# A fused recurrence and two-layer network: another order of the front, with pad copies first, a copy of x ahead of a copy of v, and a weight request moved up

## The chip, the cores and the metric

The kernel runs on one core of a Trainium2 chip. The metric is the device time of one execution in microseconds. Twelve runs of the kernel before lie between 196.32 and 199.08 us, with a median of 197.39. The engines are named as in the profile: PE is TensorE (PEld its weight loads), DVE is VectorE, ACT is ScalarE, POOL is GpSimd, SP is SyncE, which here only asks for transfers. Times inside an execution are counted from the start of its span.

## The reference

For each of 4 batches and 8 heads a state of 48 x 48 is carried through 768 steps, and its output goes through a network of two layers.

```python
for t in range(S):                                   # B, H, S, D = 4, 8, 768, 48
    kt, vt, rt = k[:, :, t], v[:, :, t], r[:, :, t]
    cur = np.einsum('bhd,bhe->bhde', u[None] * kt, vt)
    y[:, :, t] = np.einsum('bhd,bhde->bhe', rt, state + cur)
    state = w[None, :, :, None] * state + np.einsum('bhd,bhe->bhde', kt, vt)
...
x = y.transpose(0, 2, 1, 3).reshape(B * S, H * D)    # 3072 x 384
h = x @ w_in                                         # 384 x 2048
g = h * (1.0 / (1.0 + np.exp(-h)))
return g @ w_out                                     # 2048 x 384
```

## The kernel before

The sequence is cut into 6 chunks of 128 steps. A unit is one chunk of one batch, so there are 24 units; unit i is batch i mod 4 of chunk i // 4. Units 0 to 3 are chunk 0 and start from an empty state. Units are worked in pairs; the second of a pair is "crossed", which means that its masked products stand with the two halves of the partitions exchanged, and its v has to be copied crossed as well.

For each unit r, k and v are loaded (192 KB each, SP's queue, L73). PE turns r and k by transposes (L255) into a PSUM tile `att`; DVE multiplies them with powers of the decay while it takes them out (rT and kT, L261); PE multiplies them pairwise (L288) and DVE masks the result (am, L295). PE then forms y from am and v, and from the second chunk on from the state too (L305, L310). DVE adds the bonus term vu and writes y in 16 bits (y16, L338). The bonus comes from POOL and DVE: rk = r * k (L215), times u (L220), a sum on DVE (L228), and the product with v on POOL (vu, L233). For the state, POOL multiplies k with the decay to the chunk's end (kc, L223), PE multiplies it with v (sp, L322), and DVE adds the result to the decayed state (sdec on POOL, L333). ScalarE casts v (L242, and two more copies, L245 and L246, for a crossed unit).

The network's first layer needs y turned: PE transposes it (yT, L376) and ScalarE copies it to SBUF (xT, L380). Then come the matmuls with w_in (`hps`, L391), SiLU on ScalarE (L399), the matmuls with w_out (`ops`, L412), and the copy and store of the result. w_in and w_out are loaded as four quarters each by POOL's queue, with a cast to 16 bits (L84, L89); a quarter of w_in covers four of the 16 blocks of 128 hidden units. From chunk 1 on, y is turned by a DMA.

The engines run in the order of the program, each its own instructions one after the other; nothing is rescheduled. For the front (units 0 to 7) the order is written by hand as a string of words, `order` (L489 to L500). Each word issues one step, and all of its instructions go to one engine:

| Word | Step | Engine |
|---|---|---|
| T4 | turn r and k of unit 4 | PE |
| rT4, kT4 | take them out with the decay | DVE |
| A45 | products of units 4 and 5 | PE |
| am4, rd4, y164, st4 | mask, bonus sum, y, state | DVE |
| Y4, S4, yT4 | y, state product, turned y | PE |
| v164, xT4, r164 | casts and copies | ACT |
| rk4, ru4, vu4, kc4, sd4 | bonus products, decayed k, decayed state | POOL |
| L2.6, G2.6 | first layer of chunk 0, a block of batches from 2 on, hidden block 6: matmuls, then SiLU | PE, ACT |
| H0 | first layer of chunk 1, two hidden blocks of batches 0 and 1 | PE, ACT |
| i_q0, i_o0 | request of a quarter of w_in, of w_out | POOL |
| lr4, lk4, lv4 | loads of unit 4 | SP |
| pads | zeros beside the 48 columns of r and k of units 4 to 7: eight copies, L159 | ACT |
| mx, clear, wb | a mask, PSUM cleared, the decay spread | ACT, PE, PE |

A number with a star ahead of a word, as in `3*A23`, first issues so many matmuls on a tile of zeros (`spin`, L165), whose result nobody reads.

The tiles yp, yT, hps, sp, ops and those of `spin` share four PSUM buffers (tag "moe"). A new tile takes the buffer that was released earliest in the program's order: its first matmul waits until the last reader of that buffer is done. In the order before, L0.4 takes the buffer of L0.2 (free after G0.2), L4.8 that of S1 (free after st1), and yT4 that of L4.14.

After the order string a loop (L522 to L574) works the units 6 to 23 in pairs, with pieces of the two layers as fillers between them. The change doesn't touch it.

Of the kernel before, what the change touches and what calls it, by code (L numbers as in the profile page):

```python
# [15 lines left out]
def kernel(  # L16
# [132 lines left out]
    eK = cst.tile([PR, NP, C], FP)  # L149
    lamR = cst.tile([PR, NP, C], FP)  # L150
    lamK = cst.tile([PR, NP, C], FP)
    lnw_bc = cst.tile([128, HD], FP)
    lamC = cst.tile([128, H, D], FP)
# [316 lines left out]
    def piece(word, f):  # L470
# [16 lines left out]
        "lr": lambda i: ld(i, rin, r), "lk": lambda i: ld(i, kin, k), "lv": lambda i: ld(i, vin, v),  # L487
    }
    order = """  # L489
        lnw eK lamK mx clear lr4 lk4 lv4 lr5 lk5 lv5 lr6 lk6 lv6 lr7 lk7 lv7 4*T0 rk0 rT0 kT0  # L490
        1*T1 rT1 kT1 rk1 ru0 rd0 v160 v161 3*A01 wb am0 ru1 vu0 rd1 am1 vu1 lnwb lamC i_q0 1*Y0
        y160 T2 kT2 rT2 2*Y1 rk2 1*yT0 xT0 ru2 3*T3 kT3 rT3 v162 y161 rk3 i_q1 3*A23 v163 pads
        yT1 xT1 ru3 rd2 vu2 rd3 vu3 am2 am3 L0.0 G0.0 L0.2 G0.2 Y2 y162 Y3 y163 kc0 i_q2 yT2 xT2
        L0.4 G0.4 kc1 yT3 xT3 L0.6 G0.6 S0 st0 kc2 T4 kT4 rT4 kc3 L2.0 G2.0 S1 L2.2 G2.2 st1 rk4
        v164 L2.4 G2.4 S2 L2.6 G2.6 st2 ru4 i_q3 r164 L4.8 G4.8 S3 L4.9 G4.9 st3 rd4 rk5 L4.10
        G4.10 T5 kT5 rT5 L4.11 G4.11 vu4 ru5 i_o0 A45 rd5 am4 r165 v165 L4.12 G4.12 vu5 kc4
        L4.13 G4.13 am5 sd4 kc5 Y4 S4 y164 st4 L4.14 G4.14 sd5 i_o1 Y5 S5 y165 st5 L4.15 G4.15
        yT4 xT4 yT5 xT5 T6 kT6 rT6 rk6 ru6 i_o2 H0 H1 v166 r166 H2 H3 T7 kT7 rT7 rk7 i_o3 v167
        r167 H4 ru7 rd6 stb4 stb5
    """  # L500
    for word in order.split():
# [104 lines left out]
```

## Time and profile before

| What | Value |
|---|---|
| Median of 12 runs | 197.39 us (196.32 to 199.08) |
| Profiled execution | 197.65 us |
| Its span, first to last instruction | 195.9 us |
| PE matmuls busy | 184.0 us, 94% of the span |
| ACT busy | 108.6 us, 55% |
| POOL busy | 120.2 us, 61% |
| DVE busy | 102.7 us, 52% |
| Mean granted clock of PE | 0.991 |

The share of PE is a mean over stages that differ. The page gives the span in 40 slices of 4.9 us, each digit a busy share in tenths (9 is 90% or more):

```profile
PE   7897399889999999999999999999999999999994
PEld 2645277557866886665556665556655556644563
DVE  6696339784664563663772782782673464200120
ACT  5391667767744276067685066793186791179300
POOL 8779962799999966937928919919827630000000
PEclk9999889999999999999999999999999999999999
DMA  5999989899828729438439358349268111320022
```

PE's row is to be read for the front: the slices from 10 on are full. PEclk is the clock that PE was granted, and it is lower in two slices of the front. The DMA row is the busy share of the 16 DMA engines.

### The profile page before, as it was taken

To read this page: it belongs to the slowest core of one execution; us is meant where nothing else is said; L and a number is where in the kernel's file an instruction comes from. 1 tells how busy PE (TensorE), PEld (TensorE's weight loads), DVE (VectorE), ACT (ScalarE), POOL (GpSimd) and SP (SyncE) were. 2 spreads that over 40 slices of the span, in tenths; PEclk is the share of its full clock that TensorE was granted. 3 is DMA by queue.
4 is the path that set the end of the run, shared out by engine and by line. 5 is a ranking of instruction groups with operands and counts; after the bars stand their busy time and mean duration, and the time that the engine had idled before them with its cause. 6 is when DMAs were issued, how large, how long until landed. Compare 5 with 4: busy or idle time off the path is not lost.

```text
span 195.9 us, 5624 instructions
## 1 busy us (share of the span) xinstructions
PE 184.0 (94%) x2306; PEld 118.5 (60%) x2306; DVE 102.7 (52%) x188; ACT 108.6 (55%) x212; POOL 120.2 (61%) x159
## 2 busy tenths in 40 slices
PE   7897399889999999999999999999999999999994
PEld 2645277557866886665556665556655556644563
DVE  6696339784664563663772782782673464200120
ACT  5391667767744276067685066793186791179300
POOL 8779962799999966937928919919827630000000
PEclk9999889999999999999999999999999999999999
DMA  5999989899828729438439358349268111320022
GB/s 105 213 176 183 215 136 208 170 179 201 124 57 179 190 62 195 130 89 165 116 61 206 103 126 176 80 87 219 64 147 196 23 23 40 84 80 0 3 80 80
DMA packets 90267, 24.35 MB, mean 124 GB/s; under 512 B 83329, under 2 KB 90242, under 8 KB 90242
## 3 DMA queue, kind: packets, MB, share of 16 engines
q1 hardware_dynamic: 85136, 20.59, 48.5%
q0 software_dynamic: 3712, 3.15, 10.7%
q8 instruction: 18, 0.29, 0.7%
q10 hardware_dynamic: 1394, 0.26, 0.7%
q14 instruction: 7, 0.06, 0.1%
HBM read 20.65 MB, written 4.72 MB: 129 GB/s over the span
## 4 chain that ended last, share of the span: by engine, by line
PE 75%; SPq 9%; DMA 5%; POOL 4%; issue 3%; ACT 2%; DVE 1%; POOLq 0%
PE ops L412 31%; PE hps L391 26%; SPq L73 8%; PE att L288 7%; DMA kin<-in_k_dram 5%; PE att L255 4%; PE yp L310 2%; PE yp L305 2%; PE sp L322 1%; PE ops L437 1%; ACT gT L399 1%; POOL kc L223 1%; SPq L110 1%; POOL vu L233 1%; POOL rk L215 1%
## 5 line engine op out<-in xcount | busy, mean ns | idle before, releaser
L391 PE MATMUL hps<-xT,win 128*128 128x512 f16 (+1 forms) x360 | 69.4, 341 | 5.2 <-ACT xT L380 5.0
L399 ACT ACTIVATE gT<-hps 128x512 f16<-128x512 f32 x96 | 56.2, 598 | 20.2 <-PE hps L391 18.1
L412 PE MATMUL ops<-wout,gT 128*128 128x384 f16 x368 | 64.0, 326 | 0.0
L391 PEld LDWEIGHTS <-win 128*128 128x128 f16 x360 | 33.8, 99 | 29.3 <-issue 4.7
L412 PEld LDWEIGHTS <-gT 128*128 128x128 f16 x368 | 34.7, 98 | 22.2
L233 POOL TENSOR_TENSOR vu<-vin,rku 128x384 f32<-128x384 f32 x24 | 19.8, 831 | 31.0 <-DVE rku L228 31.0
L418 ACT COPY osb<-ops 128x384 f32<-128x384 f32 x20 | 9.6, 479 | 43.4 <-PE ops L412 39.7
L295 DVE TENSOR_TENSOR am<-att,maskM 128x1024 f16<-128x1024 f32 x12 | 14.7, 1224 | 32.4 <-PE att L288 32.4
L215 POOL TENSOR_TENSOR rk<-kin,rin 128x384 f32<-128x384 f32 x24 | 24.1, 1005 | 3.6 <-DMA kin<-in_k_dram 3.6
L220 POOL TENSOR_TENSOR rku_f<-rk,u_bc 128x384 f32<-128x384 f32 x24 | 24.0, 1001 | 2.0 <-DMA u_bc<-in_u_dram 0.4
L223 POOL TENSOR_TENSOR kc<-kin,lamC 128x384 f16<-128x384 f32 x24 | 23.9, 1002 | 0.0
L338 DVE TENSOR_TENSOR y<-yp,vu 128x384 f16<-128x384 f32 x24 | 13.2, 555 | 18.1 <-PE yp L310 7.8
L288 PEld LDWEIGHTS att<-rT,kT 48*64 48x64 f32 x768 | 17.9, 133 | 6.6 <-issue 4.3
L288 PE MATMUL att<-rT,kT 48*64 48x128 f32 (+1 forms) x768 | 20.5, 248 | 1.3 <-DVE rT L261 1.0
L261 DVE TENSOR_TENSOR rT<-att,lamR 112x512 f32<-112x512 f32 x24 | 16.4, 684 | 9.3 <-ACT gT L399 4.0
L261 DVE TENSOR_TENSOR kT<-att,lamK 112x512 f32<-112x512 f32 x24 | 16.4, 682 | 3.6 <-PE att L255 3.5
L242 ACT CAST v<-vin 128x384 f16<-128x384 f32 x24 | 11.5, 511 | 7.4 <-DMA vin<-in_v_dram 7.4
L295 DVE TENSOR_TENSOR am<-att,maskX 128x1024 f16<-128x1024 f32 x12 | 14.6, 1213 | 0.0
L228 DVE TENSOR_REDUCE rku<-rku_f 128x8 f32<-128x384 f32 x24 | 12.4, 543 | 2.5 <-POOL rku_f L220 2.5
L333 POOL TENSOR_TENSOR sdec<-st,wCT 112x384 f32<-112x384 f32 x16 | 13.2, 827 | 0.0
L276 ACT CAST rT<-rT 112x512 f16<-112x512 f32 x20 | 12.4, 619 | 0.3 <-DVE rT L261 0.2
L420 DVE COPY osb<-ops 128x384 f32<-128x384 f32 x3 | 1.7, 557 | 19.8 <-PE ops L412 19.8
(64 smaller groups left out, 168.6 us busy)
## 6 DMA issues: line engine op xcount, KB each, us to landing
rin<-in_r_dram SPq DMA_DIRECT2D x24, 192.0 KB, 4.1
vin<-in_v_dram SPq DMA_DIRECT2D x24, 192.0 KB, 4.1
kin<-in_k_dram SPq DMA_DIRECT2D x23, 192.0 KB, 4.1
out_dram<-osb SPq DMA_DIRECT2D x23, 192.0 KB, 2.2
win<-in_moe_w_in_dram POOLq DMA_DIRECT2D x4, 384.0 KB, 6.7
wout<-in_moe_w_out_dram POOLq DMA_DIRECT2D x4, 384.0 KB, 6.1
xT<-y SPq DMA_TRANSPOSE x18, 2.3
kin<-in_k_dram ACTq DMA_DIRECT2D x1, 192.0 KB, 3.8
```

The lines of the kernel that those rows point to most:

```text
L73: eng.dma_start(out=dst[i % NIN][:, :, 0:D], in_=src[b, :, sc * C:sc * C + C, :].rearrange("h t d -> t h d"))
L215: nc.gpsimd.tensor_tensor(out=L(i)["rk"], in0=kin[i % NIN][:, :, 0:D], in1=rin[i % NIN][:, :, 0:D], op=ALU.mult)
L220: nc.gpsimd.tensor_tensor(out=L(i)["rku_f"], in0=L(i)["rk"], in1=u_bc, op=ALU.mult)
L223: nc.gpsimd.tensor_tensor(out=kc[i % NIN][:, :, 0:D], in0=kin[i % NIN][:, :, 0:D], in1=lamC, op=ALU.mult)
L233: nc.gpsimd.tensor_tensor(out=L(i)["vu"], in0=vin[i % NIN], in1=L(i)["rku"].unsqueeze(2).broadcast_to([128, H, D]), op=ALU.mult)
L261: nc.vector.tensor_tensor(out=L(i)[key].rearrange("p g (y t) -> p y g t", y=2), in0=L(i)["t"][0:PR, :, x], in1=lam.rearrange("p g (y t) -> ...
L288: nc.tensor.matmul(a[e][o0:o0 + HC, j, p, c0:C], kT[r0:r0 + D, p, s0:s0 + HC], rT[r0:r0 + D, p, c0:C], start=True, stop=True)
L295: nc.vector.tensor_tensor(out=am.rearrange("p h g c -> p (h g) c"), in0=L(i)["a"].rearrange("p h g c -> p (h g) c"), in1=(maskX if crossed ...
L333: nc.gpsimd.tensor_tensor(out=L(i)["sdec"], in0=st[b], in1=wCT.unsqueeze(2).broadcast_to([PR, NP, PW]), op=ALU.mult)
L391: nc.tensor.matmul(hps[:, f, :], win[:, q, (ft + f) * 128:(ft + f + 1) * 128], xts[sc][:, q, b0:b0 + nb, :].rearrange("p b t -> p (b t)"), ...
L399: nc.scalar.activation(out=gts[sc][:, ft:ft + m, b0 * C:(b0 + nb) * C], in_=hpss[b0, ft], func=AF.Silu)
L412: nc.tensor.matmul(opss[b], gts[sc][:, ft, b * C:(b + 1) * C], wout[:, ft, :], start=(ft == 0), stop=(ft == NFT - 1))
```

## The change

Only the order string is changed; no instruction is altered, and three matmuls of zeros are added. Part by part:

- `pads` stands after `mx` on ScalarE instead of after `v163`.
- `i_q0`, the request of the first quarter of w_in, stands ahead of `vu1` on POOL instead of after it.
- `yT1 xT1` stand ahead of `v163`, so that ScalarE copies unit 1's x before it casts unit 3's v.
- `3*` stands ahead of `L0.0`: three matmuls of zeros on PE. They take one more turn of the shared PSUM buffers.
- `T5 kT5 rT5` stand ahead of `L4.10` on PE. DVE's order stays as it was.
- `kc5` stands ahead of `sd4` on POOL.
- `yT4 xT4` stand ahead of `L4.15`, and `G4.15` after `xT5` on ScalarE. By the order of releases yT4 now takes the buffer of S4 (free after st4), and L4.15 that of L4.14.

```diff
-        lnw eK lamK mx clear lr4 lk4 lv4 lr5 lk5 lv5 lr6 lk6 lv6 lr7 lk7 lv7 4*T0 rk0 rT0 kT0
-        1*T1 rT1 kT1 rk1 ru0 rd0 v160 v161 3*A01 wb am0 ru1 vu0 rd1 am1 vu1 lnwb lamC i_q0 1*Y0
-        y160 T2 kT2 rT2 2*Y1 rk2 1*yT0 xT0 ru2 3*T3 kT3 rT3 v162 y161 rk3 i_q1 3*A23 v163 pads
-        yT1 xT1 ru3 rd2 vu2 rd3 vu3 am2 am3 L0.0 G0.0 L0.2 G0.2 Y2 y162 Y3 y163 kc0 i_q2 yT2 xT2
-        L0.4 G0.4 kc1 yT3 xT3 L0.6 G0.6 S0 st0 kc2 T4 kT4 rT4 kc3 L2.0 G2.0 S1 L2.2 G2.2 st1 rk4
-        v164 L2.4 G2.4 S2 L2.6 G2.6 st2 ru4 i_q3 r164 L4.8 G4.8 S3 L4.9 G4.9 st3 rd4 rk5 L4.10
-        G4.10 T5 kT5 rT5 L4.11 G4.11 vu4 ru5 i_o0 A45 rd5 am4 r165 v165 L4.12 G4.12 vu5 kc4
-        L4.13 G4.13 am5 sd4 kc5 Y4 S4 y164 st4 L4.14 G4.14 sd5 i_o1 Y5 S5 y165 st5 L4.15 G4.15
-        yT4 xT4 yT5 xT5 T6 kT6 rT6 rk6 ru6 i_o2 H0 H1 v166 r166 H2 H3 T7 kT7 rT7 rk7 i_o3 v167
+        lnw eK lamK mx pads clear lr4 lk4 lv4 lr5 lk5 lv5 lr6 lk6 lv6 lr7 lk7 lv7 4*T0 rk0 rT0
+        kT0 1*T1 rT1 kT1 rk1 ru0 rd0 v160 v161 3*A01 wb am0 ru1 vu0 rd1 am1 i_q0 vu1 lnwb lamC
+        1*Y0 y160 T2 kT2 rT2 2*Y1 rk2 1*yT0 xT0 ru2 3*T3 kT3 rT3 v162 y161 rk3 i_q1 3*A23 yT1
+        xT1 v163 ru3 rd2 vu2 rd3 vu3 am2 am3 3*L0.0 G0.0 L0.2 G0.2 Y2 y162 Y3 y163 kc0 i_q2 yT2
+        xT2 L0.4 G0.4 kc1 yT3 xT3 L0.6 G0.6 S0 st0 kc2 T4 kT4 rT4 kc3 L2.0 G2.0 S1 L2.2 G2.2 st1
+        rk4 v164 L2.4 G2.4 S2 L2.6 G2.6 st2 ru4 i_q3 r164 L4.8 G4.8 S3 L4.9 G4.9 st3 rd4 rk5 T5
+        kT5 rT5 L4.10 G4.10 L4.11 G4.11 vu4 ru5 i_o0 A45 rd5 am4 r165 v165 L4.12 G4.12 vu5 kc4
+        L4.13 G4.13 kc5 am5 sd4 Y4 S4 y164 st4 L4.14 G4.14 sd5 i_o1 Y5 S5 y165 st5 yT4 xT4 L4.15
+        yT5 xT5 G4.15 T6 kT6 rT6 rk6 ru6 i_o2 H0 H1 v166 r166 H2 H3 T7 kT7 rT7 rk7 i_o3 v167
```

## The prediction

> **What bounds the kernel now.** I read the page's slices first: PE is 9 tenths busy from slice 10 (49 us) to the end, so a later us is bought only with matmul work, which the change leaves alone. The holes are in slices 1 to 9. Next the waits, who for whom, of 16 to 54 us (total, times, longest):
>
> ```profile
> POOL vu L233 <- DVE rku L228: 5.3, 1, 5.3
> PE hps L391 <- ACT xT L380: 5.0, 2, 4.5
> DVE y L338 <- PE yp L310: 4.9, 2, 4.6
> ...
> ACT v L242 <- DMA vin<-in_v_dram: 3.7, 1, 3.7
> ```
>
> One wait of 4.5 us of PE for ScalarE's copy xT, and DVE waiting 4.6 us for PE after it. The timeline of PE and then of ScalarE shows why (start, us, instruction, idle before):
>
> ```profile
> 18.07 0.34 PE L376 MATMUL yT<-ident,y 128*128 128x128 f16 x3
> 22.87 2.72 PE L391 MATMUL hps<-xT,win 128*128 128x256 f16 x12 [4.46 <-ACT xT L380]
> 25.39 0.52 PE L310 MATMUL yp<-v,am 128*128 128x48 f16 x8
> ...
> 26.81 0.82 PE L391 MATMUL hps<-xT,win 128*128 128x256 f16 x6
> ```
>
> ```profile
> 15.00 0.51 ACT L242 CAST v<-vin 128x384 f16<-128x384 f32 x1 [0.53 <-DMA vin<-in_v_dram]
> 19.17 0.51 ACT L242 CAST v<-vin 128x384 f16<-128x384 f32 x1 [3.65 <-DMA vin<-in_v_dram]
> ...
> 20.76 0.30 ACT L159 CAST rin<-idle 128x128 f32<-128x128 f16 x1
> ...
> 22.36 0.47 ACT L380 COPY xT<-yT 128x384 f16<-128x384 f16 x1
> ```
>
> Unit 1's y was turned at 18.07 + 0.34 = 18.41; its copy ran at 22.36, behind unit 3's v (landing awaited to 19.17, then three instructions) and eight pad copies. The delay from 18.45 (yT0 ended at 13.96, xT0 began at 14.00) is 3.91 = 0.72 waiting for v + 1.59 v work + 1.60 pads. Third, the windows (length, busy time of PE, PEld, DVE, ACT, POOL, clock, DMA share, GB/s):
>
> ```profile
> 18.40:22.80 4.40, 0.01 (x1) 0.10 (x1) 2.81 (x3) 3.57 (x12) 4.38 (x6) 0.98 1.24 227
> 22.80:26.00 3.20, 3.13 (x27) 2.33 (x27) 0.00 (x0) 0.99 (x3) 3.12 (x5) 0.50 1.14 195
> ...
> 28.30:37.00 8.70, 7.99 (x91) 5.30 (x88) 8.04 (x21) 6.35 (x13) 2.29 (x3) 1.00 1.03 184
> ...
> 44.30:53.50 9.20, 8.94 (x144) 7.37 (x144) 5.34 (x8) 7.43 (x14) 9.08 (x13) 1.00 1.08 167
> ```
>
> After the empty stretch PE ran 3.2 us at clock 0.50. From 28.3 to 37.0 DVE is the chain (8.04 of 8.70 busy), and the DMA share is above 1 almost throughout, so transfers are what the earlier PE can run into.
>
> **The change, part by part.** Letters and unit numbers are the order's words.
>
> *xT1 ahead of v163, pads first.* xT1 runs 18.45 to 18.93 and L0.0 starts at 18.97 instead of 22.87: 3.90. The pads, 8 x 0.20 = 1.60, go where ScalarE stood idle from 6.01 to 9.09 (3.08 us waiting for unit 0's v); without that cover they would cost 1.60. The loads of units 4 to 7, queued on SP at 13.44 and later, find them done. v163 is then free at 18.93, before its data (19.15), so it ends at 20.75 as before.
>
> *Clock.* L0.0 and L0.2 took 25.39 - 22.87 = 2.52 at half clock. At full clock six such matmuls take 0.66 (26.81 to 27.47), twelve 1.32. With the empty stretch gone 1.20 more is saved: PE passes L0.2 at 20.29 instead of 25.39.
>
> *Three warm matmuls ahead of L0.0.* At the 0.21 pace of their 0.82 us group they fill 18.24 to 18.88, inside the wait for xT1: nothing. If xT1 were ready at once they would cost 0.64.
>
> *What is late next.* Y2 and Y3 need am3 (ends 21.45 before) and unit 3's crossed v (20.75); y162 then ends near 21.95. ScalarE's G0.0 and G0.2 follow v163: 20.75 + 2 x 0.60 = 21.95, which frees L0.4's buffer. So L0.4 can't start before 22.0 (26.81 before): 4.8 gained at most. L0.4 also needs w_in quarter 1, and here POOL's order counts:
>
> ```profile
> 10.21 0.83 POOL L233 TENSOR_TENSOR vu<-vin,rku 128x384 f32<-128x384 f32 x1
> 12.05 0.83 POOL L233 TENSOR_TENSOR vu<-vin,rku 128x384 f32<-128x384 f32 x1 [1.00 <-DVE rku L228]
> 12.82 0.93 POOL L84 DMA_DIRECT2D win<-in_moe_w_in_dram  x1
> ...
> 16.77 0.80 POOL L84 DMA_DIRECT2D win<-in_moe_w_in_dram  x1
> ```
>
> *Quarter 0 ahead of vu1.* The request's 0.93 fits the 1.00 that POOL idled before vu1 (11.04 to 11.97, when rd1 ends), so vu1 stays at 12.05 and everything behind it on POOL moves up 0.9: quarter 1 is asked for at 15.85, quarter 2 at 20.15. The four quarters took 5.1, 6.3, 7.1 and 8.0 us from issue to landing, median 6.7: quarter 1 lands between 20.95 and 23.85, I take 22.55 (24.77 before). L0.4 then starts at 22.6: **4.2 gained**. Ends: 4.8 if it lands before 22.0; 2.0 if it lands at 24.77 as now, because shared transfers give nothing back. Quarter 0 itself (landed at 19.12) would hold L0.0 by 0.15 at worst.
>
> The loads of this stretch took 3.6 to 4.6 us to land before the first quarter was under way (units 2 and 3) and 6.3 to 9.7 with quarters in flight: the quarter that comes earlier is paid for by the loads of v. [...]
>
> *S0 to A45.* S0 follows L0.4 by 1.48 as before (28.29 - 26.81) at 24.1. From S0 to A45 (8.7 us, to 37.0) DVE works through its own order, so the 4.2 is carried. Its inputs: quarter 2, 20.15 + 5.1 to 8.0 = 25.3 to 28.2, for L4.8 at 32.50 - 4.2 = 28.3; unit 5's k landed at 29.28. T5, now ahead of L4.10, comes to PE near 29.8, and DVE wants it at 35.65 - 4.2 = 31.45 less T5's 0.7: k of unit 5 may be 1.4 late at no cost. The move itself gains nothing, since kT5 (35.65) directly followed rd4 and never waited for T5.
>
> *kc5 ahead of sd4, yT4 and yT5 around L4.15.* S5 waited for kc5 to 41.84; kc5 comes 0.82 earlier, sd4 0.99 later, so st4 (41.34) would wait to 41.8 and y165 end near 43.1 in the old times; yT5 0.34, xT5 0.48 and steps between them give H0 at 44.05 against 44.27: 0.2 gained. Ends: +0.5 (only kc5's side counts) and -0.45 (only st4's). L4.15 fills PE meanwhile.
>
> *Sum.* 4.2 + 0.2 = 4.4. From H0 on PE is busy 8.94 of 9.20, then always, so the shift reaches the end. The profiled execution took 197.65 (span 195.9 and 1.75 around it): 193.25. The median of the runs is 197.39, 0.26 less: **193.0**. Own range, by the ends above: 192.1 to 195.6.
>
> **Rivals.**
> 1. *Transfers don't come earlier*: quarter 1 lands at 24.77. 2.0 + 0.2 = 2.2: **195.2**. For: DMA share 1.24 in that stretch. Against: quarter 1 had to follow quarter 0 on its queue, which now starts 1.8 earlier.
> 2. *Given back at w_out*: its last quarter was asked for at 47.16, landed 6.4 later at 53.56, and first used at 55.54, only 2.0 of slack. If the transfers as a whole can't end before 53.5, that use moves to 53.55 instead of 51.1, and 2.0 is left: **195.4**. For: share 1.08 from 44.3 on. Against: POOL asks 4.4 earlier too, and 26 to 28 us had a share of 0.76.
> 3. *Slower: unit 3's v starved.* vu3 stands in POOL's queue ahead of kc0 and quarter 2's request. Should both quarters go ahead of v3, it lands after quarter 1's latest 23.85 plus 192 KB at 227 GB/s, 0.85: 24.7; vu3 0.83 and kc0 0.95 put the request at 26.5, landing 7.1 later at 33.6, while L4.8 used it at 32.50: 1.1 lost, **198.5**. It decides from v3 at 23.6 on. Against: v3 landed at 19.15 with quarter 0 in flight, and quarter 1 isn't asked for before 15.85.
> 4. *It doesn't do what it says*: the gap between L0.2 and L0.4 (20.3 to 22.6) brings the half clock back. One stretch as now costs 1.2: **194.2**. The 2.3 us are half of the 4.46 that led to it.
>
> **How the numbers follow.** Forecast 0.50; rivals 1 and 2 together 0.28, rival 4 0.10, rival 3 0.07; 0.05 for an end near 197. A measurement of this kernel tells from no change about 0.5%, 1.0 us: faster is below 196.4. Faster: 0.50 + 0.28 + 0.10 = 0.88; same 0.05; slower 0.07. The range takes the forecast's upper end (4.8 + 0.5 gained, 192.1, and 0.3 for runs) and reaches past rivals 1 and 2: 191.8 to 195.8.
>
> **What would show it.** Right: xT1 within 0.1 of yT1's end, L0.0 near 19.0, no clock of 0.50 around 23 to 26, L0.4 at 22 to 23 waiting for win's landing, H0 near 39.9. Wrong: L0.4 at 24.8 (rival 1); ops stalled for wout near 51 to 53 (rival 2); vu3 waiting for vin past 23 (rival 3); T3 later than 14.6, which would mean that quarter 0 held up unit 3's k and the whole front.

## The result, and the profile after

The changed kernel took 194.56 us (median of 15 runs, 192.71 to 196.44) against 198.29 of the kernel before (63 runs, 196.20 to 200.18): a ratio of 0.9818, 95% interval 0.979 to 0.9846. The ratios leave out the runs that lie more than 1.5% above the fastest of their kernel, the medians do not. The profiled execution went from 197.65 to 192.79 us, its span from 195.9 to 191.1, its mean clock from 0.991 to 1.000. So the two profiles differ by 4.9 us and the medians by 3.7; the section on the prediction takes that difference apart as far as the runs allow.

The slices of the profile after (40 of 4.8 us, busy share in tenths):

```profile
PE   7999998899999999999999999999999999999993
...
PEclk9999999999999999999999999999999999999999
DMA  5999999999959377269195287276386201320022
```

The hole in PE's row (a 3 in slice 4 before) is gone, and so are the two 8s in PEclk's row. The timeline of PE after, around unit 1's turned y (start, us, instruction, idle before it and what ended it):

```profile
18.51 0.34 PE L376 MATMUL yT<-ident,y 128*128 128x128 f16 x3
18.68 0.81 PE L165 MATMUL zs<-idle 128*128 128x512 f16 x3
19.41 1.47 PE L391 MATMUL hps<-xT,win 128*128 128x256 f16 x12
...
21.81 0.34 PE L376 MATMUL yT<-ident,y 128*128 128x128 f16 x3 [0.40 <-DVE y L338]
22.00 0.82 PE L391 MATMUL hps<-xT,win 128*128 128x256 f16 x6
...
23.48 0.33 PE L322 MATMUL sp<-v,kc 128*128 128x96 f16 x4
```

L0.0 starts 0.90 after yT1 instead of 4.80, with the zeros in between. L0.0 and L0.2 take 1.31 (19.41 to 20.72) instead of 2.52. L0.4 comes at 22.00 without a wait of its own: what PE waits for now is y of unit 2, 0.40 us. ScalarE's timeline shows the new order:

```profile
6.00 0.30 ACT L159 CAST rin<-idle 128x128 f32<-128x128 f16 x1
...
9.15 1.17 ACT L242 CAST v<-vin 128x384 f16<-128x384 f32 x2 [1.46 <-DMA vin<-in_v_dram]
...
18.28 0.51 ACT L242 CAST v<-vin 128x384 f16<-128x384 f32 x1 [3.58 <-DMA vin<-in_v_dram]
18.88 0.48 ACT L380 COPY xT<-yT 128x384 f16<-128x384 f16 x1
19.26 0.52 ACT L242 CAST v<-vin 128x384 f16<-128x384 f32 x1
...
20.86 1.09 ACT L399 ACTIVATE gT<-hps 128x512 f16<-128x512 f32 x2
```

The eight pad copies begin at 6.00, and the wait for unit 0's v that follows has shrunk from 3.08 to 1.46 us: they cost nothing. The copy xT1 starts at 18.88, directly behind v162, and v163 follows it. One line is new: v162 waits 3.58 us for a load that landed at 18.26, where before it landed at 14.98. Unit 2's v now lands after w_in's first quarter (17.48). In this execution it didn't matter, but by 0.06 us only: v162 ended at 18.79, and xT1 could not have started before 18.85. The last line is the SiLU of L0.0 and L0.2, which ends at 21.95. POOL's timeline shows the requests of the quarters:

```profile
11.09 0.93 POOL L84 DMA_DIRECT2D win<-in_moe_w_in_dram  x1
12.28 0.82 POOL L233 TENSOR_TENSOR vu<-vin,rku 128x384 f32<-128x384 f32 x1 [0.27 <-DVE rku L228]
...
16.23 0.80 POOL L84 DMA_DIRECT2D win<-in_moe_w_in_dram  x1
```

Quarter 0 filled the time in which POOL had waited for rd1. Quarter 1 was requested 0.54 earlier than before and landed 5.1 after its request, at 21.34 instead of 24.76.

The milestones, all from PE's timelines (us from the start of the span):

| | before | after | difference |
|---|---|---|---|
| yT1 starts | 18.07 | 18.51 | +0.44 |
| L0.0 | 22.87 | 19.41 | -3.46 |
| L0.4 | 26.81 | 22.00 | -4.81 |
| S0 | 28.29 | 23.48 | -4.81 |
| A45, after rT5 | 37.00 | 32.18 | -4.82 |
| H0 | 44.27 | 39.35 | -4.92 |
| span | 195.95 | 191.06 | -4.89 |

The whole gain is made between yT1 and L0.4 and then carried to the end. The waits of 12 to 53 us after (total, times, longest):

```profile
ACT v L242 <- DMA vin<-in_v_dram: 3.6, 1, 3.6
...
POOL vu L233 <- DVE rku L228: 1.6, 2, 1.4
...
DVE y L338 <- PE yp L310: 1.2, 3, 0.7
...
DVE st L349 <- POOL sdec L333: 0.4, 1, 0.4
PE yT L376 <- DVE y L338: 0.4, 1, 0.4
PE hps L391 <- DVE st L349: 0.4, 1, 0.4
```

The wait of PE for xT and the 4.6 us of DVE for PE have gone. Two waits of 0.4 are new, both from the edit of the tail: st4 waits for sd4, and PE for st4.

### The profile page after: what moved, and what is told of

Its sections match the earlier page's. It is cut to its first block, busy times and chain, and to the rows that moved or that the text cites. A ratio compares the mean times of both kernels' runs of the same rounds, so it can differ in the third digit from the quotient of the medians.

```text
span 191.1 us, 5631 instructions
## 1 busy us (share of the span) xinstructions
PE 184.1 (96%) x2309; PEld 118.4 (62%) x2309; DVE 102.8 (54%) x188; ACT 108.7 (57%) x212; POOL 120.2 (63%) x159
## 3 DMA queue, kind: packets, MB, share of 16 engines
q0 software_dynamic: 3712, 3.15, 11.3%
HBM read 20.65 MB, written 4.72 MB: 133 GB/s over the span
## 4 chain that ended last, share of the span: by engine, by line
PE 77%; SPq 11%; POOL 3%; DMA 3%; issue 2%; ACT 1%; DVE 1%; POOLq 0%
PE ops L412 32%; PE hps L391 27%; SPq L73 10%; PE att L288 7%; PE att L255 5%; DMA kin<-in_k_dram 3%; PE yp L310 2%; PE yp L305 2%; PE ops L437 1%; PE sp L322 1%; POOL kc L223 1%; ACT gT L399 1%; SPq L110 1%; POOL vu L233 1%; POOL rk L215 1%
## 5 line engine op out<-in xcount | busy, mean ns | idle before, releaser
L391 PE MATMUL hps<-xT,win 128*128 128x512 f16 (+1 forms) x360 | 68.2, 337 | 0.6 <-DVE st L349 0.4
L391 PEld LDWEIGHTS <-win 128*128 128x128 f16 x360 | 33.3, 98 | 24.6 <-issue 1.3
L412 PEld LDWEIGHTS <-gT 128*128 128x128 f16 x368 | 34.7, 98 | 22.2
L295 DVE TENSOR_TENSOR am<-att,maskX 128x1024 f16<-128x1024 f32 x12 | 14.6, 1214 | 0.0
```

The source lines that it names most:

```text
L295: nc.vector.tensor_tensor(out=am.rearrange("p h g c -> p (h g) c"), in0=L(i)["a"].rearrange("p h g c -> p (h g) c"), in1=(maskX if crossed ...
L391: nc.tensor.matmul(hps[:, f, :], win[:, q, (ft + f) * 128:(ft + f + 1) * 128], xts[sc][:, q, b0:b0 + nb, :].rearrange("p b t -> p (b t)"), ...
L412: nc.tensor.matmul(opss[b], gts[sc][:, ft, b * C:(b + 1) * C], wout[:, ft, :], start=(ft == 0), stop=(ft == NFT - 1))
```

## The experiments

The ratio of an experiment is to runs of the kernel before on the same chip in the same series; the four times to the right come from one profiled execution, which can lie anywhere among the runs of its kernel (the fastest of six for the copy of x alone, the slowest of twelve for the pads alone, the slowest of six for the second run with the quarter back). One measure is of use in all of them: the time from yT1 to H0, which leaves out how late yT1 itself was in that execution. It was 26.20 before and 20.84 after.

| kernel | ratio to before, 95% | yT1 | L0.0 | L0.4 | H0 | yT1 to H0 |
|---|---|---|---|---|---|---|
| before | | 18.07 | 22.87 | 26.81 | 44.27 | 26.20 |
| before, again | one run | 20.76 | 23.68 | 27.60 | 45.06 | 24.30 |
| after | 0.9818 (0.979 to 0.9846) | 18.51 | 19.41 | 22.00 | 39.35 | 20.84 |
| after, again | 0.9811 (0.9763 to 0.9859) | 17.86 | 18.77 | 21.49 | 38.84 | 20.98 |
| copy of x alone | 0.9887 (0.9829 to 0.9946) | 18.27 | 19.18 | 22.51 | 39.98 | 21.71 |
| pads alone | 0.9925 (0.9895 to 0.9955) | 18.02 | 21.57 | 25.62 | 43.91 | 25.89 |
| copy and pads | 0.9874 (0.9835 to 0.9912) | 17.96 | 18.87 | 23.51 | 42.33 | 24.37 |
| after, quarter back | 0.9809 (0.9764 to 0.9855) | 18.15 | 19.06 | 22.64 | 39.99 | 21.84 |
| the same again | 0.9882 (0.9834 to 0.9931) | 21.07 | 21.98 | 24.57 | 41.89 | 20.82 |
| after, pads back | 0.9818 (0.9756 to 0.9879) | 18.04 | 19.23 | 22.08 | 39.91 | 21.87 |
| after, tail back | 0.9815 (0.975 to 0.9879) | 18.26 | 19.17 | 21.90 | 39.36 | 21.10 |
| after, other tail | 0.985 (0.9796 to 0.9904) | 18.14 | 19.05 | 22.14 | 39.46 | 21.32 |
| after, no zeros | 0.9813 (0.974 to 0.9886) | 18.35 | 19.26 | 22.00 | 39.35 | 21.00 |
| before, wait filled | 1.0042 (1.0 to 1.0084) | 20.47 | 24.96 | 27.54 | 44.98 | 24.51 |

**The copy of x alone.** The kernel before, with nothing but `yT1 xT1` moved.

```diff
-... 3*A23 v163 pads yT1 xT1 ru3 ...
+... 3*A23 yT1 xT1 v163 pads ru3 ...
```

> The order before, with one edit: unit 1's turn and copy of x (yT1 xT1) ahead of unit 3's v; pads stay behind v163, quarter 0 of w_in behind vu1, no other edit. Theory (quarter 1 is the next bound): L0.0 at 19.0 to 19.4, no stretch at clock 0.50, but L0.4 waits for quarter 1 of w_in, which lands at 24 to 25 as before (24.77), so L0.4 at 24.8 instead of 26.81 and the time 2.0 us (1.0%) below the kernel before. Rival (ScalarE's pads are the next bound): G0.0 behind the pads at 22.4, L0.4 at 23.6 with no wait for w_in, 3.2 us (1.6%) below. Rival (the copy of x is all): as the whole change, 3.6 us (1.8%) below.

It took 195.14 us (ratio 0.9887). In the profile the span is 191.7 with a clock of 1.000 throughout; H0 is at 39.98, 4.29 of the 4.92 us. PE and one line of DVE:

```profile
19.18 1.47 PE L391 MATMUL hps<-xT,win 128*128 128x256 f16 x12 [0.57 <-ACT xT L380]
...
22.51 0.81 PE L391 MATMUL hps<-xT,win 128*128 128x256 f16 x6 [0.29 <-DVE y L338]
```

```profile
18.55 0.55 DVE L228 TENSOR_REDUCE rku<-rku_f 128x8 f32<-128x384 f32 x1 [0.89 <-POOL rku_f L220]
```

So in this profile the one move holds most of the gain, the half clock included. By the times it holds less, 1.1 of the 1.8%: the profile is the fastest of six runs, and four of the six kept the clock (0.998 or more, median 194.38). The theory named the wrong next bound: quarter 1, asked for at 16.68 as before, landed at 22.43 and not at 24 to 25. The 0.5 us that L0.4 still lacks is not the pads': they hold G0.0 up to 22.23, but L0.4 waits for DVE, and y163 ends at 22.46 (DVE's timeline). DVE is late because am3 ends at 21.36 and not at 20.97, behind rd3, which waits 0.89 for ru3 on POOL, and ru3 starts at 17.50 and not at 17.06. The request of a quarter stands ahead of it on POOL. So a second effect of the quarter's place shows here: it moves DVE's masks. The late mask is not alone, though: with quarter 1 landing at 22.43, L0.4 could have come only some 0.03 earlier here.

**The quarter back, twice.** The whole change, but with `i_q0` where it was.

```diff
-... am1 i_q0 vu1 lnwb lamC 1*Y0 ...
+... am1 vu1 lnwb lamC i_q0 1*Y0 ...
```

> The whole change except that the request of quarter 0 of w_in goes back behind vu1 and lamC on POOL. Theory (the earlier request buys the landing of quarter 1): quarter 1 asked for near 16.8 again, landing 24 to 25, L0.4 waits for it, 1.5 to 2.7 us slower than the whole change, so 1.0% below the kernel before. [...]

> The whole change with the request of quarter 0 of w_in behind vu1 again (as e2_quarter_back), once more: so far it gave 0.981 and a wait of 0.26 for quarter 1, while the copy, pads and zeros without the quarter and the tail gave 0.987 and a wait of 1.31. Theory (the earlier request is worth something, because quarter 1 lands between 22.5 and 24.8 without it): L0.4 waits for w_in by 0.3 to 2, ratio 0.983 to 0.988, half-clock stretches in a third or more of the runs. Rival (it is worth nothing, and the difference lay in the runs drawn): ratio 0.979 to 0.983, L0.4 within 0.7 of the whole change (22.0 and 21.5).

The first time 193.94 us (6 runs), the second 195.36 (6 runs); the intervals of the two ratios overlap. In the first profile quarter 1 was requested at 16.84, landed at 22.60, and L0.4 waited 0.26 for it. In the second L0.4 did not wait for it, because the whole front was 2.9 us late. The second run's timeline of PE shows where that began:

```profile
13.82 0.44 PE L255 MATMUL att<-ident,kin 64*112 64x64 f32 x8 [1.59 <-DMA kin<-in_k_dram]
...
21.07 0.34 PE L376 MATMUL yT<-ident,y 128*128 128x128 f16 x3
...
21.98 1.47 PE L391 MATMUL hps<-xT,win 128*128 128x256 f16 x12
```

PE waited 1.59 for unit 2's k, the 3.41 us from 14.47 on ran at clock 0.50, and yT1 came at 21.07. From yT1 on this execution is as short as the changed kernel (20.82). What the quarter is worth is therefore not settled by the times: the twelve runs together have a median of 194.3, the 22 of the changed kernel 194.1, and three of the twelve lost the clock for a stretch against five of those 22. The profiles show two differences. Quarter 1 lands at 21.0 to 22.1 in the six profiles with the early request, and at 22.2 to 23.5 in the four that have xT1 ahead and the late one; L0.4 waited for it 0 to 0.35 in the first group, and 0 to 1.31 in the second. In four of the first six (the second profile of the changed kernel, the tail back, the other tail, no zeros) L0.4 started 0.05 after quarter 1 had landed, so the quarter was the bound, or close to it, there too. And ru3 starts on POOL at 16.44 to 17.06 in the first group, at 17.48 to 17.74 in the second, so that am3, where k was in time, ends at 20.3 to 21.0 or at 21.3 to 21.5. Where k was in time, L0.4 came at 21.49 to 22.14 with the early request and at 22.51 to 23.51 with the late one.

**The pads back.** The whole change, but with the pads behind `v163`.

```diff
-... mx pads clear ... yT1 xT1 v163 ru3 ...
+... mx clear ... yT1 xT1 v163 pads ru3 ...
```

> The whole change except that the eight pad copies go back on ScalarE behind unit 3's v (so now between v163 and G0.0). Theory: G0.0 starts 1.6 later, at 22.4, G0.2 ends near 23.5 and frees L0.4's buffer, L0.4 at 23.6 instead of 22.0: 1.5 us slower than the whole change. Rival (ScalarE has slack here): the same as the whole change within 0.5 us.

194.08 us, the same ratio as the whole change. In the profile L0.4 is at 22.08; the delay shows one step later, where L0.6 waits 0.15 for G0.2 and S0 comes at 24.04, 0.56 after that of the whole change. In this build the buffers are paired in another way, and L0.4 escapes the late SiLU.

**The tail back.** The whole change, without its edits of T5, kc5 and yT4 to L4.15.

```diff
-... rk5 T5 kT5 rT5 L4.10 G4.10 L4.11 ... kc5 am5 sd4 ... yT4 xT4 L4.15 yT5 xT5 G4.15 T6 ...
+... rk5 L4.10 G4.10 T5 kT5 rT5 L4.11 ... am5 sd4 kc5 ... L4.15 G4.15 yT4 xT4 yT5 xT5 T6 ...
```

> The whole change except that its three later parts are undone: T5 behind L4.10, sd4 ahead of kc5, L4.15 and G4.15 ahead of yT4 as before. Theory: within 0.5 us of the whole change (0.1 slower by the trace: S0 to H0 took 15.98 before and 15.87 after); S5 waits for kc5 again, DVE's st4 no longer for sd4 (0.4). Rival (these parts carry some of the gain): 0.5 to 1 us slower than the whole change.

194.66 us. From S0 to H0 it took 15.97 us against 15.87: the edits of the tail are worth 0.1 us, below what the times can tell.

**Another tail.** The whole change, with both state updates behind y of unit 5, and L4.15 behind both turned y, meant to take away both new waits of 0.4.

```diff
-... y164 st4 L4.14 G4.14 sd5 i_o1 Y5 S5 y165 st5 yT4 xT4 L4.15 yT5 xT5 G4.15 T6 ...
+... y164 L4.14 G4.14 sd5 i_o1 Y5 S5 y165 st4 st5 yT4 xT4 yT5 xT5 L4.15 G4.15 T6 ...
```

> The changed kernel with another tail: on DVE y165 ahead of st4 and st5, on PE yT5 ahead of L4.15, G4.15 behind L4.15. Theory: yT5 no longer waits for st4 and st5, nor L4.15 for st4 between the two turns (0.40): both turns by 37.4, the copies of x by 38.3, H0 at 38.8 instead of 39.35: 0.5 us below the changed kernel in the trace, 0.3%, at the edge of what times tell. Rival (the state added later delays kT6 and what follows): the same or 0.3 slower.

194.2 us, S0 to H0 15.84 us: nothing gained. The timeline of PE in the changed kernel shows the wait that the edit takes away:

```profile
37.08 0.33 PE L376 MATMUL yT<-ident,y 128*128 128x128 f16 x3
37.81 0.81 PE L391 MATMUL hps<-xT,win 128*128 128x512 f16 x3 [0.40 <-DVE st L349]
38.46 0.33 PE L376 MATMUL yT<-ident,y 128*128 128x128 f16 x3
```

yT4 did not wait for st4: it had a buffer that ScalarE freed at 37.04, and L4.15 had the one that st4 frees. In the other tail yT5 does come earlier, right behind yT4 at 37.23, but L4.15 then starts at 38.13 instead of 37.81, and H0 follows 2.66 after S5 instead of 2.69. The pieces changed places; the last of them ended when it had before.

**Both kernels again.** The same two kernels on one chip, to see how far one profile can be trusted.

> The kernel before once more, for a second profile. The two profiles in hand differ by 4.9 us, the timed runs by 3.6. Theory (the first profile of before is an ordinary one, the gain in it real): unit 1's copy of x at 22.3 to 22.4 again, clock 0.50 for some 3.4 us, L0.4 near 26.8, span 195.5 to 196.3. Rival (part of the 4.9 is an accident of that execution): the half clock is absent or shorter, or unit 3's v lands earlier than 19.15, L0.4 at 25.6 or earlier, span 194.5 or less.

> The changed kernel once more, for a second profile and more times. Theory: L0.0 at 19.0 to 19.5, L0.4 at 22 to 22.5, H0 at 39 to 40, ratio to the kernel before 0.979 to 0.985. Rival (its front depends on the landings and its first profile was a lucky one): unit 2's or unit 3's v, or quarter 1, lands 0.5 to 2 us later, L0.4 at 23 or later, span above 192.

The changed kernel: 193.73 us (6 runs), span 190.5, clock 1.000, L0.4 at 21.49. The kernel before: one run of 198.5, span 196.8, clock 0.983, and in it the accident already seen:

```profile
13.55 0.68 PE L255 MATMUL att<-ident,kin 64*112 64x64 f32 x8 [1.15 <-DMA kin<-in_k_dram]
...
20.76 0.34 PE L376 MATMUL yT<-ident,y 128*128 128x128 f16 x3
23.68 2.69 PE L391 MATMUL hps<-xT,win 128*128 128x256 f16 x12 [2.58 <-ACT xT L380]
```

yT1 is 2.69 later than in the first profile of this kernel, but L0.0 only 0.81: the rest went into the wait for xT1, which shrank from 4.46 to 2.58. Where xT1 goes first there is no such wait to take it up: between the two profiles with the quarter back, yT1 differs by 2.92, L0.0 by 2.92 and the span by 2.5 (191.7 and 194.2); L0.4 and H0 differ by only 1.9, because in the first of them L0.4 waited for quarter 1. Against the first profile of the changed kernel the late one has yT1 2.57 and H0 2.54 later.

**The pads alone.** The kernel before, with the pads moved and nothing else.

```diff
-... eK lamK mx clear ... 3*A23 v163 pads yT1 ...
+... eK lamK mx pads clear ... 3*A23 v163 yT1 ...
```

> The order before, with one edit: the eight pad copies first on ScalarE. Unit 1's copy of x stays behind unit 3's v, so it runs at 20.76 instead of 22.36 and L0.0 at 21.3. Theory (the half clock follows an empty stretch of about 4.2 us: it began at 22.59, 4.18 after the last matmul at 18.41): the stretch is 2.9 us, the clock stays at 1.00, 1.6 + 1.2 are saved, L0.4 near 24.0, 2.8 us (1.4%) below the kernel before. Rival (2.9 us is enough to lose the clock): 1.6 us (0.8%) below, with a stretch at 0.50. Rival (only the copy's place counts): no difference.

196.18 us, ratio 0.9925. xT1 comes at 21.04, 1.32 earlier. The clock was lost all the same, and in the profiled execution, the slowest of the twelve runs, for twice as long (mean clock 0.983; eight of the twelve runs have 0.991, one stretch). The windows of 3.41 us (length, busy time of PE, PEld, DVE, ACT, POOL, clock, DMA share, GB/s):

```profile
17.08:20.49 3.41, 1.28 (x53) 1.13 (x44) 2.23 (x4) 1.01 (x2) 3.16 (x5) 1.00 1.25 230
20.49:23.90 3.41, 2.33 (x12) 1.60 (x12) 0.90 (x1) 1.59 (x4) 3.39 (x4) 0.50 1.24 217
23.90:27.32 3.42, 3.02 (x31) 2.45 (x30) 1.02 (x2) 1.25 (x3) 3.34 (x5) 0.50 1.21 218
```

**The wait filled with zeros.** The kernel before, with 20 matmuls of zeros ahead of L0.0, to keep the clock up while xT1 is waited for.

```diff
-... am2 am3 L0.0 G0.0 ...
+... am2 am3 20*L0.0 G0.0 ...
```

> The kernel before with one edit: twenty matmuls of zeros (20 x 0.213 = 4.3 us) ahead of L0.0, in the time in which PE waits for unit 1's copy of x; ScalarE's order stays as before. It tells the clock's share of the gain from the order's. Theory (the half clock is a price of its own: so far a stretch of 3.41 us ran at half clock after each one in which PE was busy 2.33 us or less): L0.0 still near 22.9, clock 1.00 from 22 to 26, L0.4 at 25.6 instead of 26.8, mean clock 0.991 or above in nearly all runs, 1.2 to 1.7 us (0.6 to 0.9%) below the kernel before. Rival (what is late behind L0.0 hides the clock): the same as the kernel before within 0.5 us. Rival (the matmuls of zeros push the rest): slower.

198.61 us, ratio 1.0042. This failed as a measure of the clock. In the profiled execution k of unit 2 was late again (a wait of 1.09), yT1 came at 20.47, and the zeros, 4.48 us from 20.65 on, held L0.0 until 24.96 although xT1 was there at 23.42. The clock was kept after yT1 (mean 0.991, one stretch at 0.50, from 13.07 to 16.49), and L0.0 to L0.4 took 2.58 instead of 3.94; what the zeros saved there they cost ahead of it. The times say a little more: five of the twelve runs kept the clock at 1.000 throughout, and their median, 197.41, is no better than the 196.97 of the runs of the kernel before that lost one stretch (table below). That speaks against 1.2 us as a gain of its own on the path, but no such run was profiled, and the zeros may have held L0.0 in them too.

**No zeros.** The whole change without the three matmuls of zeros.

```diff
-... am2 am3 3*L0.0 G0.0 ...
+... am2 am3 L0.0 G0.0 ...
```

> The whole change without the three matmuls of zeros ahead of L0.0. Theory: PE stands still for 0.6 us there, L0.0 at the same time after yT1 (0.90), the profile and the times as the whole change (ratio 0.979 to 0.985). Rival (they keep the clock): half-clock stretches in more of the runs than the 5 of 22 of the whole change, 1 us slower.

193.23 us, L0.0 0.91 after yT1 as with them, where PE now waits 0.57. They are worth nothing that shows.

**Copy and pads.** The kernel before with the pads first, xT1 ahead and the three zeros, but neither the quarter nor the tail.

```diff
-... am1 i_q0 vu1 lnwb lamC 1*Y0 ...
+... am1 vu1 lnwb lamC i_q0 1*Y0 ...
...
-... T5 kT5 rT5 L4.10 G4.10 L4.11 ... kc5 am5 sd4 ... yT4 xT4 L4.15 yT5 xT5 G4.15 T6 ...
+... L4.10 G4.10 T5 kT5 rT5 L4.11 ... am5 sd4 kc5 ... L4.15 G4.15 yT4 xT4 yT5 xT5 T6 ...
```

(The diff is against the changed kernel.)

> The kernel before with three of the seven edits: pads first, unit 1's copy of x ahead of unit 3's v, three matmuls of zeros ahead of L0.0; the requests of w_in and the later parts as before. Theory (these carry the gain): L0.0 at 19.0 to 19.4, L0.4 at 22.3 to 22.9 waiting for quarter 1 up to 0.6, span within 0.8 us of the whole change, ratio 0.979 to 0.987. Rival (the quarter's earlier request or the tail is needed): L0.4 at 24 or later, 2 us slower than the whole change.

195.13 us (12 runs), ratio 0.9874. Here quarter 1 landed at 23.47, PE waited 1.31 for it, and the 3.41 us from 23.76 on ran at clock 0.50:

```profile
18.87 1.47 PE L391 MATMUL hps<-xT,win 128*128 128x256 f16 x12
...
23.51 1.26 PE L391 MATMUL hps<-xT,win 128*128 128x256 f16 x6 [1.31 <-DMA win<-in_moe_w_in_dram]
24.57 0.53 PE L376 MATMUL yT<-ident,y 128*128 128x128 f16 x3
```

S0 came at 26.18, 2.70 later than in the changed kernel. This is what the prediction's rivals 1 and 4 describe, a late quarter 1 (if not as late as 24.77) and a half clock after the gap between L0.2 and L0.4, in a kernel that lacks the quarter's move.

None of these kernels is measurably faster than the changed one.

## Why the prediction was right, and where not

**The copy.** Forecast: L0.0 at 18.97, 3.90 gained. Measured: 0.90 from yT1 to L0.0, as forecast, but yT1 was 0.44 later, so 19.41 and 3.46. T3 began at 14.76, past the 14.6 that was named as a sign of quarter 0 holding up the front. Over the undisturbed profiles yT1 lies between 17.86 and 18.51 with the quarter early and between 17.96 and 18.27 with it late, so the quarter has not been shown to be the cause. Half of the 0.44 was there before it was asked for at 11.09: DVE's rT0 starts at 7.56 instead of 7.34.

**The clock.** Forecast 1.20 for L0.0 and L0.2; measured 2.52 less 1.31, 1.21.

**L0.4's floor and quarter 1.** L0.4 stood at the floor of 22.0. Two bounds meet there: the SiLU of L0.2, whose buffer L0.4 was to take, ended at 21.95, as worked out, and yT2, which stands 0.19 ahead of L0.4 on PE, waited 0.40 for y162. The profile names the second; whether the first held L0.4 at all is not shown. The lines of DVE, the mask am3 and y:

```profile
19.76 1.21 DVE L295 TENSOR_TENSOR am<-att,maskX 128x1024 f16<-128x1024 f32 x1
21.19 1.02 DVE L338 TENSOR_TENSOR y<-yp,vu 128x384 f16<-128x384 f32 x2 [0.21 <-PE yp L310]
```

The step that failed in size was "I take 22.55" for the landing, from the median of 6.7 us: quarter 1 was asked for at 16.23 and not at 15.85, but came after 5.1 and landed at 21.34, inside the range given (20.95 to 23.85). So L0.4 gained 4.81, not 4.2. The 24.77 that it was set against was itself an outlier: in the seven other profiles with the late request quarter 1 landed between 22.2 and 23.6. The prediction also followed only the quarter's request up POOL's queue. It said that everything behind quarter 0 moves up there, and didn't follow ru3, which moves with it and brings am3 forward from 21.45 to 20.97. And it put nothing between y162 and L0.4, where yT2 stands: with am3 at 21.45 and y162 near 21.95, L0.4 would have come near 22.2. That the floor came out at 22.0 is in part the luck of two things left out. In the second profile of the changed kernel L0.4 came at 21.49, 0.05 after quarter 1 landed. That the loads of v pay for the earlier quarter, as the prediction has it, does show: unit 2's v landed at 18.26 instead of 14.98, 3.28 us later. ScalarE waited 3.58 us for it and POOL 0.32, and neither held up PE.

**S0 to the end.** The 4.8 us were carried through DVE's chain to A45 (4.82) as forecast, and T5's move gained nothing, as forecast. For the tail 0.2 was forecast and 0.1 measured. The buffers were not as the description of the change says: yT4 again took that of L4.14, and L4.15 that of S4. The pairing is therefore not to be read off the order of words; it changed even when only the pads moved (with the pads back, L0.4 starts at 22.08, while the SiLU of L0.2 runs until 23.34).

**The rivals.** Rival 1 did not come about in the changed kernel; with copy and pads alone quarter 1 did come late, at 23.47. Rival 2 (w_out) did not: no matmul of ops waited for wout, and the last quarter landed at 49.6, a us ahead of its first use. Rival 3 did not: vu3 ended at 20.0, and L4.8 waited 0.20, for the state and not for a transfer. Rival 4 did not in either profile of the changed kernel, neither of which has a clock of 0.50 from 7.1 us on; but five of its 22 runs lost one stretch, and where it lay in them is not known.

**The sum.** The forecast gained 4.4 and gave 193.0; the profiles gained 4.9, the medians 3.7, and the time was 194.56, inside the range. Part of the 1.56 us is that the kernel before had a median of 198.29 over 63 runs instead of the 197.39 shown. The rest, 0.66, is that the medians differ by 3.73 and not by 4.4: the sum took its differences from one execution of the kernel before, and as undisturbed. (Its own upper end is a slip as well: 2.0 less 0.45 gives 195.8 and not 195.6.) The runs by their mean clock show what was left out (the kernel before by the 62 runs taken beside the experiments); one stretch of 3.41 us at 0.50 takes 0.009 from the mean:

| | runs | mean clock | median us |
|---|---|---|---|
| after (both series) | 17 | 0.998 or more | 193.76 |
| after (both series) | 5 | 0.991 | 195.29 |
| before | 23 | 0.991 | 196.97 |
| before | 39 | 0.983 or less | 198.19 |

None of these runs of the kernel before kept the clock. In the better row of each the kernels differ by 3.2 us. The profiled execution of the kernel before lay 0.7 above its row's median, that of the changed one 1.0 below: 3.2 + 0.7 + 1.0 = 4.9, the difference of the profiles. In the worse rows they differ by 2.9. One mechanism that the profiles show is the late k of unit 2, which struck in three of them: the kernel before hid most of it under the wait for xT1 (one profile), and the order with xT1 first passes it on (one profile, with the quarter back). There the removed wait had been the cover of another delay. It is not the only way to a lower clock: the pads alone lost two stretches with k in time. How large a share of the 1.2 us between profiles and medians this makes was not measured: only single profiles show where the time went.

**Open.** What the clock alone is worth on the path (the filled wait failed to separate it in its profile, and its times give it no gain), and what the quarter's move is worth in the median.

## What to carry to other kernels

Before a copy that the bottleneck waits for, look at what its engine's queue holds and which of that waits for a load: here moving one pair of words held 4.3 of 4.9 us in the profiles, and 1.1 of 1.8% in the times. Work the gain out to the next bound (here a SiLU and y of unit 2, 22.0) rather than adding up the stretches that shorten. And don't expect the median to gain as much as a pair of clean profiles: a wait that goes may have been cover for whatever comes late ahead of it.

## What was not expected of the hardware

**In these profiles the half clock came in stretches of 3.41 us, one or two in a row, and one of them came after a stretch without an idle time of PE over 1.15 us.** The kernel before in its second profile, cut at the edges of the clock:

```profile
10.10:13.51 3.41, 2.12 (x33) 1.03 (x25) 3.34 (x5) 3.27 (x7) 2.73 (x4) 1.00 0.91 181
13.51:16.92 3.41, 3.37 (x25) 1.85 (x25) 1.43 (x3) 1.37 (x3) 3.31 (x5) 0.50 0.87 137
16.92:20.34 3.42, 3.16 (x67) 2.00 (x69) 2.41 (x5) 0.62 (x2) 1.85 (x3) 1.00 1.24 223
20.34:23.75 3.41, 0.83 (x34) 0.64 (x28) 2.62 (x3) 3.24 (x12) 3.39 (x5) 1.00 1.17 211
23.75:27.16 3.41, 3.26 (x28) 2.36 (x27) 0.36 (x1) 1.19 (x2) 3.41 (x4) 0.50 0.89 130
```

The column to read is PE's busy time, the second, against the clock of the next row. After 2.12 and 0.83 busy of 3.41 the next stretch is at 0.50; after 3.37 and 3.16 it is at 1.00. In the first row PE's longest idle time was 1.15 us. With the pads alone, a stretch of 1.28 was followed by 0.50, and one of 2.33, itself at 0.50, again by 0.50. But busy time alone did not decide it. The first two rows are from the filled wait, the third from the first profile of the kernel before:

```profile
9.66:13.07 3.41, 2.47 (x52) 1.38 (x45) 3.29 (x5) 3.06 (x8) 2.69 (x4) 1.00 1.02 204
13.07:16.49 3.42, 3.10 (x24) 1.86 (x25) 1.78 (x4) 1.42 (x2) 3.32 (x4) 0.50 0.80 129
15.77:19.18 3.41, 2.38 (x68) 1.82 (x68) 2.23 (x6) 0.01 (x1) 3.39 (x5) 1.00 1.17 196
```

A stretch of 2.47 busy, with PE's wait of 1.09 for unit 2's k at its end, was followed by 0.50, and one of 2.38 by 1.00. What the limit is, these profiles do not settle.

**In the late loads one of the 16 completion marks came late.** In the three profiles with the late k of unit 2, 15 of that load's 16 completion marks were there by 11.7 to 12.0 us and the last between 13.35 and 13.78. In each of the three the records have an instruction packet of 16 KB and about 0.96 us, at 11.3 to 11.5, but they don't name its DMA engine, and four profiles with k in time have such a packet at 11.3 to 11.4 too. In the first profile of the kernel before, quarter 1 had 15 of its 16 marks by 22.61 and the last at 24.76; a packet of the same kind took 2.03 us there, from 20.33; the other four in the first profiles of the two kernels took 0.88 to 1.21. That these packets are the cause was not tried and is not shown.
